# A decode step with modulation, attention and a token mixer: a quarter of two modulation terms loaded by GpSimd, and three terms formed by wide products and a fold

## The chip, the cores and the metric

The kernel runs on one core of one Trainium2 chip. The metric is the device time of one execution in microseconds. Five engines work side by side, each through its own instruction queue: TensorE (PE in the profile; its weight loads are PEld), VectorE (DVE), ScalarE (ACT), GpSimd (POOL) and SyncE (SP). Transfers between HBM and the on-chip memory (SBUF) are issued from one of these queues and carried out by 16 DMA engines. Products of TensorE land in PSUM.

## What is computed

One decoding step for four sequences (B = 4) of width D = 512:

```python
mod = (silu(c) @ w_mod).reshape(B, 6, 1, D)
sa, ca, ga, sb, cb, gb = mod[:, 0], ..., mod[:, 5]
h = layernorm(x) * (1 + ca) + sa
x = x + ga * attention(h, k_cache, v_cache, wq, wo)   # 32 query heads, 8 key/value heads, 4096 cached positions
h = layernorm(x) * (1 + cb) + sb
x = x + gb * mixer(h, w1, b1, w2, b2)                 # u = gelu(layernorm(h) * w1 + b1), y = u @ w2 + b2, hidden width 1792
```

All is float32. The caches of 4 x 8 heads are 2 MB for keys and 2 MB for values each, `w_mod` is 512 x 3072 (6.3 MB), `wq` and `wo` are 8.4 MB each: 157 MB are read once.

## The kernel before

**Items.** The attention is cut into 32 items, one for each pair of sequence and key/value head. For item `i`: `scores` (eight products against the key block), row maxima (`row_max`, `turn_max`, `col_max`, `spread_max`, `copy_max`), `expo` on ScalarE, `turn` (transposes), `sums` and `scale`, `values` (eight products in four column groups), `copy_v`, `pick`, `copy_o`, `project` with `wo`, and `add_up`. A loop runs items 0 to 23 in software-pipelined order; the last eight are put in order by a written plan (`PLAN`), in which the mixer of the last two sequences and the last modulation term are woven in.

**Transfers.** All loads are issued by SP, in the order of the code. Large ones land in a ring of three buffers of 32 KB in each lane (tag `kv`): first the weights of modulation terms 0 and 1 (`wm01`), then `wq` in two halves, the first two key blocks, and then pairs of a later key block and an earlier value block (`load_pair`, 4 MB each). A load into a ring buffer waits, on SP's queue, until the buffer's last reader is done; everything behind it on SP waits too. `wo` comes in four pieces into buffers of its own. At the end come single key and value blocks, the last value block in four pieces, and last the weights of modulation term 5 (`load_wm5`).

**Small inputs.** `small` holds in each of 128 lanes the mixer's `w1`, `b1`, `w2` (14 columns each), the 16 columns of `c` transposed, and `b2`. It is loaded at the start in three pieces (lanes 0 to 6, 6 to 16, 16 to 128), `x` behind it. `w1n`, the negative of `w1`, is VectorE's first instruction (L70); the constants follow. `sg`, `sT` and `sT8` (L118 to L125) are silu(c), the last repeated eight times so that each sequence fills eight rows of a product.

**The modulation terms.** Terms 0 and 1 are made at the start. Terms 2, 3 and 4 are made in the loop at i = 2 (L609 to L616): `load_wm24` (L197), called at i = 1 behind the load of a pair and a piece of `wo`, brings their weights, 3 x 1 MB, into one ring buffer. `mod(t)` makes one term as [128, 128], sixteen products of [128 x 32] by [128 x 128]: four quarters `k` of the 512 inputs, and four blocks `c` of the 512 outputs, each block in its own group of 32 PSUM rows. The term is copied into `prep`. The PSUM buffer for this (pool `ps_e`) is a single one.

**Elsewhere.** `fold_groups` (L355) sums the four row groups of a [128, 512] accumulator by products with the column `first`, and gives [128, 128]. The buffers `u` (three of [128, 2, 512]) belong to the mixer, whose first instance starts at i = 8. GpSimd makes the identity at the start (in `make_identity`) and has nothing else to do.

Of the kernel before, what the change touches and what calls it, by code (L numbers as in the profile page):

```python
# [8 lines left out]
F32 = mybir.dt.float32  # L9
I32 = mybir.dt.int32  # L10
AF = mybir.ActivationFunctionType
OP = mybir.AluOpType
# [9 lines left out]
NSM = 3 * NF + 16 + 1  # L22

# [5 lines left out]


@with_exitstack
def adaln_decode(ctx: ExitStack, tc: tile.TileContext, small, x, wmod, wq, kk, kv, vv, wo, out):
# [16 lines left out]
    sm = cst.tile([P, NSM], F32, name="sm")  # L51
    xr = wk.tile([P, D], F32, name="xr", tag="yw", bufs=1)[0:B]
    wm01 = ring.tile([P, 2, 4, D], F32, name="wm01", tag="kv")
    nc.sync.dma_start(wm01, wmod[0])
# [9 lines left out]
    cT = sm[:, 3 * NF:3 * NF + 16]  # L64
    b2 = sm[:, 3 * NF + 16:]
# [4 lines left out]
    dv.tensor_scalar(w1n, w1, -1.0, None, op0=OP.mult)  # L70
    ones = cst.tile([P, P], F32, name="ones")
    dv.memset(ones, 1.0)
    dv.memset(neg1, -1.0)
# [4 lines left out]
    g32 = cst.tile([P, 32], F32, name="g32")  # L78
# [9 lines left out]
    first = g32[:, 0:1].to_broadcast([P, 32])  # L88
# [8 lines left out]
    sT8 = cst.tile([P, 4, B, 8], F32, name="sT8")  # L97

    def rsqrt(ve, n, tag, beside=None, out=None, times=None):
        y = wk.tile([n, 1], F32, name="y" + tag)  # L100
# [11 lines left out]
        if times is not None:  # L112
# [2 lines left out]
        dv.scalar_tensor_tensor(y, q, RS3, y, op0=OP.add, op1=OP.mult)  # L115
        return y

    sg = cst.tile([P, 16], F32, name="sg")  # L118
    nc.scalar.activation(sg, cT, AF.Exp, scale=-1.0)
    dv.tensor_scalar(sg, sg, 1.0, None, op0=OP.add)  # L120
    dv.reciprocal(sg, sg)
    sT = cst.tile([P, 4, B], F32, name="sT")
    dv.tensor_mul(sT.rearrange("p k b -> p (k b)"), sg, cT)  # L123
    dv.tensor_copy(sT8.rearrange("p k b r -> p (k b) r"),
                   sT.rearrange("p k b -> p (k b)").unsqueeze(2).to_broadcast([P, 16, 8]))  # L125

    st = wk.tile([B, 6], F32, name="st0")
    dv.bn_stats(st, xr)
# [59 lines left out]
    def load_pair(i):  # L188
        t = slots()
        nc.sync.dma_start(t, kv[i])  # L190
        key(t[:, 0], i + 2)
        value(t[:, 1], i)

    def load_wo(h):
        nc.sync.dma_start(wo_p[h // 2], wo[h // 2])

    def load_wm24():  # L197
        w = ring.tile([P, 3, 4, D], F32, name="wm24", tag="kv")
        nc.sync.dma_start(w[:, 0:2], wmod[1])
        nc.sync.dma_start(w[:, 2], wmod[2][:, 0])  # L200
        for e in range(3):
            WM[2 + e] = w[:, e]

    def load_wm5():
        t = slots().rearrange("p s (k n) -> p (s k) n", n=D)
        nc.sync.dma_start(t[:, 0:4], wmod[2][:, 1])
        WM[5] = t[:, 0:4]
        return t[:, 4:6]

    def load_key(t, i):  # L210
# [9 lines left out]
    def modmm(pm, t, ks=range(4)):  # L220
        for k in ks:
            for c in range(4):
                mm(pm[32 * c:32 * c + 32, :], sT8[:, k].rearrange("p b r -> p (b r)"),
                   WM[t][:, k, c * P:(c + 1) * P], start=(k == 0), stop=(k == 3))

    def mod(t):
        pm = ps_e.tile([P, P], F32, name=f"pm{t}", tag="e")
        modmm(pm, t)
        return pm

    S, M, PL, SEL = {}, {}, {}, {}

    def scores(i):
        b, h = divmod(i, HKV)
        S[i] = s = ps_s.tile([P, 1024], F32, name=f"s{i}", tag="s")
        for n in range(2):
            for c in range(4):
                mm(s[32 * c:32 * c + 32, n * 512:(n + 1) * 512], QT[:, b, h, :],  # L238
                   KT[i][:, (n * 4 + c) * 512:(n * 4 + c + 1) * 512], start=True, stop=True)
# [91 lines left out]
    def project(i, pa=None):  # L331
        b, h = divmod(i, HKV)
        oT = OT.pop(i)
        if pa is None:
            pa = ps_m.tile([P, D], F32, name="pa", tag="m")
            for g in range(REP):
                mm(pa[32 * g:32 * g + 32, :], oT[:, g:g + 1].to_broadcast([P, 32]), wo_t[h][:, g, :],  # L337
                   start=True, stop=True)
        else:
            for g in range(REP):  # L340
                for c in range(4):
                    mm(pa[32 * c:32 * c + 32, :], oT[:, g:g + 1].to_broadcast([P, 32]),
                       wo_t[h][:, g, c * P:(c + 1) * P], start=(g == 0 and h == HKV - 2),
                       stop=(g == REP - 1 and h == HKV - 1))
        PA[i] = pa
# [6 lines left out]
        else:  # L352
            dv.tensor_add(ACC[b], ACC[b], pa)  # L353

    def fold_groups(pool, acc, tag):  # L355
        pc = pool.tile([P, P], F32, name="pc", tag=tag)
        for c in range(4):
            mm(pc[32 * c:32 * c + 32, :], first, acc[:, c * P:(c + 1) * P], start=True, stop=True)
        return pc

    def residual(x1, pc):
# [216 lines left out]
    for i in range(NS - HKV):  # L578
        load_pair(i + 1)
        if i in (1, 3, 5):  # L580
            load_wo(i + 1)
        if i == 1:
            load_wm24()
        scores(i + 2)
        row_max(i + 2)
        if i:
            pick(i - 1)
            copy_o(i - 1)
        turn(i + 1)
        sums(i + 1)  # L590
        scale(i + 1)
        if i:
            project(i - 1)
            add_up(i - 1)
        turn_max(i + 2)
        col_max(i + 2)
        values(i, range(4))
        spread_max(i + 2)
        copy_max(i + 2)
        expo(i + 2)  # L600
        if i and i % HKV == 0:
            mix = Mixer(i // HKV - 1)
        if mix:
            mix.inner(i % HKV)
        values(i, range(4, 8))
        copy_v(i)
        if mix:
            mix.outer(i % HKV)
        if i == 2:  # L609
            for t in range(2, 5):  # L610
                pm = mod(t)
                dst = prep[:, {2: 1, 3: 2, 4: 3}[t]]
                if t == 4:
                    dv.tensor_scalar(dst, pm, 1.0, None, op0=OP.add)
                else:
                    dv.tensor_copy(dst, pm)  # L616
        if i == NS - HKV - 2:
            gate = spread_gate()
# [25 lines left out]
    for step in PLAN.split():  # L644
        op, k = step.rstrip("0123456789."), step.lstrip("abcdefghijklmnopqrstuvwxyzABCDEFGHIJKLMNOPQRSTUVWXYZ")
        i, q = (int(n) for n in (k + ".0").split(".")[:2]) if k else (0, 0)
# [32 lines left out]
        elif op == "y":  # L679
            pc = fold_groups(ps_m, ACC.pop(B - 1), "m")  # L680
# [54 lines left out]
```

## Time and profile before

| | us |
|---|---|
| median of three timed runs | 389.92 (388.86 to 390.04) |
| the profiled execution, its span | 386.94 |
| TensorE busy | 298.9 (77%) |
| VectorE busy | 215.2 (56%) |
| ScalarE busy | 108.0 (28%) |
| GpSimd busy | 0.7 |
| DMA queue q1 (all loads) | 157.33 MB, 94.8% of 16 engines' time |

How to read the profile: the page gives busy time by engine, then the span in 40 equal slices (busy tenths, the granted TensorE clock, the busy share of the DMA engines, GB/s), then the DMA queues, and then the chain of work that ended last, followed back from the last instruction at each step to what released it. Rows of the chain have the start in us, the duration in us, and what ran. Rows of the timeline have the start, the duration, engine and line, the operation with its output and inputs, the shape, the count, and in brackets how long the engine had been idle before and what ended that. Rows of windows have busy time and count of instructions of each engine in a stretch, then the granted clock, the DMA share and GB/s. A matmul of float32 counts as two entries (x8 is four products).

### The profile page before, as it was taken

The page shows a single profiled execution, that of the slowest core. Times are in us where ns is not written, and L with a number is a line of the kernel's source. Part 1 is how long each engine was busy: PE and PEld are TensorE (multiplying, and loading weights), DVE is VectorE, ACT ScalarE, POOL GpSimd, SP SyncE. Part 2 cuts the span into 40 slices and gives each one's busy share as a digit, 9 for nine tenths or more (in the row PEclk, how much of TensorE's full clock was granted, in tenths as well). Part 3 has the DMA queues.
Part 4 walks back from the last instruction along what each step waited for, and adds up shares of the span by engine and source line. Part 5 has one row for each costly group of instructions (what it writes and reads, how often), then busy time and mean ns, then how long its engine had stood idle before and what let it go on. Part 6 is the DMA issues. An engine that isn't in the chain of part 4 may idle for free.

```text
span 386.9 us, 5714 instructions
## 1 busy us (share of the span) xinstructions
PE 298.9 (77%) x2416; PEld 122.4 (32%) x2416; DVE 215.2 (56%) x516; ACT 108.0 (28%) x132; POOL 0.7 (0%) x6
## 2 busy tenths in 40 slices
PE   0765575863966949979888859999988887999984
PEld 0111121231323313334222323443323342444562
DVE  0420351620542524676766644676875579788766
ACT  0101120110110110113567210213783104757356
POOL 0000000000000000000000000000000000000000
PEclk9998875986695775989999985978999998899999
DMA  8999999999999999999999999999999999999910
GB/s 329 430 434 434 415 451 430 410 449 432 418 447 434 430 434 432 434 432 434 426 434 429 434 429 434 434 432 434 425 434 432 434 429 434 422 427 423 404 46 3
DMA packets 7281, 157.70 MB, mean 408 GB/s; under 512 B 964, under 2 KB 980, under 8 KB 1368
## 3 DMA queue, kind: packets, MB, share of 16 engines
q1 hardware_dynamic: 7248, 157.33, 94.8%
q8 instruction: 19, 0.31, 0.3%
q14 instruction: 6, 0.05, 0.0%
q10 hardware_dynamic: 8, 0.00, 0.0%
HBM read 157.32 MB, written 0.01 MB: 407 GB/s over the span
## 4 chain that ended last, share of the span: by engine, by line
DMA 54%; PE 28%; DVE 16%; issue 1%; SPq 1%; ACTq 0%; DVEq 0%
DMA kv<-in_kv 47%; PE s L238 8%; PE pv L301 7%; DMA wq<-in_wq 6%; DVE m L243 3%; DVE p L275 3%; PE pt L324 2%; PE pa L337 2%; PE pb L258 2%; DVE uu L431 1%; DVE mx L252 1%; DVE acc L353 1%; PE qs L152 1%; PE phb L417 1%; PE pve L309 1%
## 5 line engine op out<-in xcount | busy, mean ns | idle before, releaser
L238 PE MATMUL s<-kv,QT 128*32 128x512 f32 x512 | 76.2, 715 | 35.6 <-DMA kv<-in_kv 32.6
L268 ACT ACTIVATE p<-s,nm 128x1024 f32<-128x1024 f32 x32 | 35.6, 1114 | 199.0 <-DVE nm L263 198.9
L243 DVE TENSOR_REDUCE m<-s 128x1 f32<-128x1024 f32 x32 | 39.2, 1224 | 76.1 <-PE s L238 76.0
L301 PE MATMUL pv<-kv,p 128*32 128x512 f32 x496 | 75.0, 684 | 0.4 <-DMA kv<-in_kv 0.4
L275 DVE STREAM_TRANSPOSE p<-p 128x512 f32<-128x512 f32 x64 | 41.9, 687 | 1.7 <-ACT p L268 1.7
L324 PEld LDWEIGHTS pt<-sel,po 128*128 128x128 f32 x250 | 33.6, 208 | 28.7 <-issue 15.6
L238 PEld LDWEIGHTS s<-kv,QT 128*32 128x32 f32 x512 | 16.3, 125 | 81.3 <-DMA kv<-in_kv 45.3
L337 PE MATMUL pa<-wo,oT 128*32 128x512 f32 x240 | 35.3, 663 | 4.3 <-DVE oT L329 4.2
L324 PE MATMUL pt<-sel,po 128*128 128x4 f32 x250 | 36.2, 268 | 1.4 <-DVE po L315 1.4
L315 DVE COPY po<-pv 128x512 f32<-128x512 f32 x31 | 21.4, 689 | 17.0 <-PE pv L301 17.0
L252 DVE TENSOR_REDUCE mx<-pm 1x128 f32<-1x512 f32 x32 | 21.4, 671 | 0.8 <-PE pm L247 0.7
L258 PEld LDWEIGHTS pb<-neg,mx 1*128 1x128 f32 x64 | 10.8, 210 | 32.9 <-DVE mx L252 31.1
L487 ACT ACTIVATE u<-u 128x1024 f32<-128x1024 f32 x20 | 20.4, 1052 | 2.7 <-DVE u L431 2.6
L431 DVE TENSOR_SCALAR u<-hb,wr,sm 128x512 f32<-128x512 f32 x40 | 19.9, 541 | 1.0 <-PE py L442 0.9
L353 DVE TENSOR_TENSOR acc<-acc,pa 128x512 f32<-128x512 f32 x26 | 17.7, 681 | 3.6 <-PE pa L337 3.6
L268 ACT ACT_TABLE_LOAD x11 | 14.1, 1283 | 19.0 <-DVE nm L263 18.9
L137 PE MATMUL s<-wm,sT 128*4 128x512 f32 x16 | 8.4, 684 | 12.2 <-DVE sT L123 12.2
L258 PE MATMUL pb<-neg,mx 1*128 1x1 f32 x64 | 13.5, 278 | 5.3 <-DVE mx L252 5.3
L487 ACT ACT_TABLE_LOAD x13 | 16.7, 1283 | 0.2
L247 PE MATMUL pm<-ident,m 128*1 128x128 f32 x32 | 9.1, 286 | 9.8 <-DVE rl L284 3.8
L301 PEld LDWEIGHTS pv<-kv,p 128*32 128x32 f32 x496 | 14.1, 146 | 8.1 <-issue 2.1
L247 PEld LDWEIGHTS pm<-ident,m 128*1 128x1 f32 x32 | 2.5, 80 | 39.1 <-DVE rl L284 21.0
(144 smaller groups left out, 212.3 us busy)
## 6 DMA issues: line engine op xcount, KB each, us to landing
kv<-in_kv SPq DMA_DIRECT2D x28, 4096.0 KB, 20.8
wq<-in_wq SPq DMA_DIRECT2D x2, 4096.0 KB
wo<-in_wo SPq DMA_DIRECT2D x4, 2048.0 KB
kv<-in_kv SPq DMA_DIRECT2D x4, 2048.0 KB, 18.5
wm<-in_wmod SPq DMA_DIRECT2D x2, 2048.0 KB
kv<-in_kk SPq DMA_DIRECT2D x1, 4096.0 KB
kv<-in_vv SPq DMA_DIRECT2D x3, 1024.0 KB
wm<-in_wmod SPq DMA_DIRECT2D x1, 1024.0 KB
```

Of the source, the lines that this page charges most:

```text
L238: mm(s[32 * c:32 * c + 32, n * 512:(n + 1) * 512], QT[:, b, h, :], KT[i][:, (n * 4 + c) * 512:(n * 4 + c + 1) * 512], start=True, stop=True)
L243: dv.tensor_reduce(M[i], S[i], axis=AX.X, op=OP.max)
L252: dv.tensor_reduce(mx, M[i].rearrange("o (c r) -> o r c", c=4).unsqueeze(1).to_broadcast([1, 4, 32, 4]), axis=AX.X, op=OP.max)
L258: mm(pb, M[i].rearrange("o c r -> o (c r)"), neg1, start=True, stop=True)
L268: nc.scalar.activation(p, S[i], AF.Exp, bias=M.pop(i), accum_out=l)
L275: dv.transpose(p, p)
L301: mm(PV[i][32 * q:32 * q + 32, :], pT[:, 128 * k:128 * k + 128:4], VT[i][:, 4 * k:4 * k + 4, :].rearrange("p j d -> p (j d)"), start=(k < ...
L324: mm(pt, po[:, c * DH:(c + 1) * DH], sel[:, c, :], start=(c == 0), stop=(c == n - 1))
L337: mm(pa[32 * g:32 * g + 32, :], oT[:, g:g + 1].to_broadcast([P, 32]), wo_t[h][:, g, :], start=True, stop=True)
L353: dv.tensor_add(ACC[b], ACC[b], pa)
L431: dv.tensor_scalar(u[:, e, :], hb, wr[:, j:j + 1], b1[:, j:j + 1], op0=OP.mult, op1=OP.add)
L487: nc.scalar.activation(u, u, AF.Gelu_apprx_tanh)
```

## The change

Five things change.

1. `small` is split. `cond` (32 columns of `c`, and `b2`) is loaded at the start in the same three pieces; `mlp` (`w1`, `b1`, `w2`) is loaded with the weights of terms 2 and 3. `w1n` is made at i = 2.
2. `x` is loaded in two halves, the first by GpSimd, the second by SP.
3. Of terms 2 and 3 the first three quarters of the inputs come by SP as before (`w23`, 1.5 MB). The last quarter, 128 inputs, is laid out over 32 lanes (8 to 31 and 64 to 71), four inputs in each: 16 KB a lane for both terms. GpSimd first sets that region of the buffer to zero on all 128 lanes, and then issues four rounds of three transfers: six lanes, two lanes, and eight lanes of `mlp` (six in the last round). The remaining lanes of `mlp` come by SP.
4. `cT` has 16 more columns: on those 32 lanes the matching inputs of `c`, zero elsewhere. `sg`, `sT` and `sT8` grow with it.
5. The weights of term 4 go into two of the mixer's `u` buffers, in two loads. `mod` is replaced by `mod_wide`: for a term 7 products (4 for term 4) of [128 x 32] by [128 x 512] in four row groups, a copy to SBUF, and a fold of the four groups with `g32`.

```diff
-    for lo, hi in ((0, 6), (6, 16), (16, P)):
-        nc.sync.dma_start(sm[lo:hi], small[lo:hi])
-    nc.sync.dma_start(xr, x)
+    for lo, hi in ((0, 6), (6, 16), (16, P)):
+        nc.sync.dma_start(cond_t[lo:hi], cond[lo:hi])
+    nc.gpsimd.dma_start(xr[0:2], x[0:2])
+    nc.sync.dma_start(xr[2:B], x[2:B])
...
     def load_wm24():
-        w = ring.tile([P, 3, 4, D], F32, name="wm24", tag="kv")
-        nc.sync.dma_start(w[:, 0:2], wmod[1])
-        nc.sync.dma_start(w[:, 2], wmod[2][:, 0])
-        for e in range(3):
-            WM[2 + e] = w[:, e]
+        w = ring.tile([P, 14, D], F32, name="wm24", tag="kv")
+        low = w[:, 6:14]
+        nc.gpsimd.memset(low, 0.0)
+        nc.sync.dma_start(w[:, 0:6], w23)
+        for e in range(4):
+            nc.gpsimd.dma_start(low[8 + e:32:4], wlow[e, 0:6])
+            nc.gpsimd.dma_start(low[64 + e:72:4], wlow[e, 6:8])
+            nc.gpsimd.dma_start(sm[8 * e:min(8 * e + 8, 30)], mlp[8 * e:min(8 * e + 8, 30)])
+        nc.sync.dma_start(sm[30:P], mlp[30:P])
+        for t in range(2):
+            WM[2 + t] = [w[:, 3 * t + k] for k in range(3)] + [low[:, 2 * s + t] for s in range(NL)]
+        WM[4] = []
+        for h in range(2):
+            u = up.tile([P, 2, D], F32, name="u")
+            nc.sync.dma_start(u, w4[h])
+            WM[4] += [u[:, k] for k in range(2)]
...
-    def mod(t):
-        pm = ps_e.tile([P, P], F32, name=f"pm{t}", tag="e")
-        modmm(pm, t)
-        return pm
+    def mod_wide(t):
+        pm = ps_e.tile([P, D], F32, name=f"pm{t}", tag="e")
+        n = len(WM[t])
+        for k, w in enumerate(WM[t]):
+            q = k % 4
+            e = k if k < 3 or n == 4 else k + 1
+            mm(pm[32 * q:32 * q + 32, :], sT8[:, e].rearrange("p b r -> p (b r)"), w, start=(k < 4), stop=(k + 4 >= n))
+        wide = wk.tile([P, D], F32, name="wide", tag="yw", bufs=1)
+        dv.tensor_copy(wide, pm)
+        return fold_groups(ps_e, wide, "e", g32)
...
-    def fold_groups(pool, acc, tag):
+    def fold_groups(pool, acc, tag, sel=None):
         pc = pool.tile([P, P], F32, name="pc", tag=tag)
         for c in range(4):
-            mm(pc[32 * c:32 * c + 32, :], first, acc[:, c * P:(c + 1) * P], start=True, stop=True)
+            mm(pc[32 * c:32 * c + 32, :], first if sel is None else sel, acc[:, c * P:(c + 1) * P], start=True, stop=True)
         return pc
...
         if i == 2:
+            dv.tensor_scalar(w1n, w1, -1.0, None, op0=OP.mult)
             for t in range(2, 5):
-                pm = mod(t)
+                pm = mod_wide(t)
```

The inputs are laid out on the host to fit:

```python
SPOT = [*range(8, 32), *range(64, 72)]
cT[SPOT, 4:] = a["c"][:, 3 * P:].reshape(B, NL, 32).transpose(2, 1, 0)
low = wm[3, :, 2:4].reshape(NL, 8, 4, 2, D)
"wlow": con(low.transpose(2, 1, 0, 3, 4).reshape(4, 8, 2 * NL, D)),
```

More of the change, by code (lines that the diff above doesn't have):

```diff
@@ L21 @@
 NS = B * HKV
-NSM = 3 * NF + 16 + 1
+NL = 4
+NC = (4 + NL) * B
+SPOT = [*range(8, 32), *range(64, 72)]
 TAU2 = (3.0 / 8.0) ** 0.4
@@ L33, in adaln_decode @@
 @with_exitstack
-def adaln_decode(ctx: ExitStack, tc: tile.TileContext, small, x, wmod, wq, kk, kv, vv, wo, out):
+def adaln_decode(ctx: ExitStack, tc: tile.TileContext, cond, mlp, x, w01, w23, wlow, w4, w5, wq, kk, kv, vv, wo, out):
     nc = tc.nc
@@ L197, in load_wm24 @@
     def load_wm24():
[L198 to L202 removed]
+        w = ring.tile([P, 14, D], F32, name="wm24", tag="kv")
[14 more added lines that the diff above has]
+            WM[4] += [u[:, k] for k in range(2)]
     def load_wm5():
         t = slots().rearrange("p s (k n) -> p (s k) n", n=D)
[L206 to L207 removed]
+        nc.sync.dma_start(t[:, 0:4], w5)
+        WM[5] = [t[:, k] for k in range(4)]
         return t[:, 4:6]
@@ L709 @@
     con = _np.ascontiguousarray
-    cT = a["c"].reshape(B, 4, P).transpose(2, 1, 0).reshape(P, 16)
-    small = _np.concatenate([
-        a["B_w1"].reshape(P, NF), a["B_b1"].reshape(P, NF), a["B_w2"].reshape(P, NF), cT,
-        _np.broadcast_to(a["B_b2"].reshape(1, 1), (P, 1))], axis=1)
+    cT = _np.zeros((P, 4 + NL, B), _np.float32)
+    cT[:, :4] = a["c"].reshape(B, 4, P).transpose(2, 1, 0)
+    cT[SPOT, 4:] = a["c"][:, 3 * P:].reshape(B, NL, 32).transpose(2, 1, 0)
+    cond = _np.concatenate([cT.reshape(P, NC), _np.broadcast_to(a["B_b2"].reshape(1, 1), (P, 1))], axis=1)
+    mlp = _np.concatenate([a["B_w1"].reshape(P, NF), a["B_b1"].reshape(P, NF), a["B_w2"].reshape(P, NF)], axis=1)
+    wm = a["w_mod"].reshape(4, P, 6, D)
+    low = wm[3, :, 2:4].reshape(NL, 8, 4, 2, D)
     k = a["A_k_cache"].reshape(B, HKV, 4, 32, 2, 16, DH).transpose(0, 1, 6, 4, 2, 5, 3)
@@ L717 @@
     arrays = {
-        "small": con(small),
+        "cond": con(cond),
+        "mlp": con(mlp),
         "x": con(a["A_x"].reshape(B, D)),
-        "wmod": con(a["w_mod"].reshape(4, P, 3, 2, D).transpose(2, 1, 3, 0, 4)),
+        "w01": con(wm[:, :, 0:2].transpose(1, 2, 0, 3)),
+        "w23": con(wm[:3, :, 2:4].transpose(1, 2, 0, 3).reshape(P, 6, D)),
+        "wlow": con(low.transpose(2, 1, 0, 3, 4).reshape(4, 8, 2 * NL, D)),
+        "w4": con(wm[:, :, 4].reshape(2, 2, P, D).transpose(0, 2, 1, 3)),
+        "w5": con(wm[:, :, 5].transpose(1, 0, 2)),
         "wq": con(a["A_wq"].reshape(2, 2, P, HQ * DH).transpose(0, 2, 1, 3)),
```

19 lines of the change are left out of this document (9 added, 10 removed).

## The prediction

> **What bounds the kernel now.** I read the page's slices first, then the queues, then the chain of waits, and then went into the last microseconds.
>
> ```profile
> span 386.9 us, 5714 instructions
> ...
> DMA  8999999999999999999999999999999999999910
> GB/s 329 430 434 434 415 451 430 410 449 432 418 447 434 430 434 432 434 432 434 426 434 429 434 429 434 434 432 434 425 434 432 434 429 434 422 427 423 404 46 3
> ...
> q1 hardware_dynamic: 7248, 157.33, 94.8%
> q8 instruction: 19, 0.31, 0.3%
> q14 instruction: 6, 0.05, 0.0%
> ```
>
> All 16 DMA engines are busy from the second slice to the 38th at about 432 GB/s, so the time is the bytes, plus a start, plus a tail of arithmetic. Of one engine: 94.8% of 16 x 386.9 us is 5869 engine-us for 157.33 MB, so 32 KB (32,768 bytes) cost an engine 1.22 us, and 16 KB 0.61 us. The nineteen packets of the q8 instruction queue take 0.3% of 16 x 386.9, or 18.6 engine-us, 0.98 us each (0.81 to 1.14 by the rounding of 0.3%), for 16 KB each: a packet from another queue holds an engine some 0.37 us longer than its bytes would (0.20 to 0.53).
>
> The chain of waits shows where the stream hands over to arithmetic:
>
> ```profile
> 271.39 18.52 DMA kv<-in_kv
> 289.95 1.97 PE s L238 x16
> ...
> 336.33 21.56 DMA kv<-in_kv
> ...
> 358.03 1.95 PE pv L301 x16
> ...
> 367.53 0.22 PE pc L358 x8
> 367.75 0.42 PE pve L309 x8
> ...
> 384.06 0.29 DVE osb L552
> ```
>
> From 358.03, when a value block lands, TensorE has no gap worth naming until the last piece of the last value block (367.75); what follows, 386.94 - 367.75 = 19.2 us, is arithmetic that the change leaves alone. A landing that comes later moves this tail by as much. A landing that comes earlier does so only if the loads before it (289.95) come earlier too; they are in the same stream, so they would.
>
> A transfer has landed only when its slowest engine is done, so I looked at how the engines finish:
>
> ```profile
> 366.00:367.00 1.00, 1.00 (x44) 0.93 (x36) 1.00 (x4) 0.82 (x1) 0.00 (x0) 1.00 0.97 389
> 367.00:368.00 1.00, 1.00 (x35) 0.64 (x31) 0.60 (x2) 0.98 (x2) 0.00 (x0) 1.00 0.61 254
> 368.00:369.00 1.00, 1.00 (x41) 0.80 (x30) 0.60 (x3) 0.74 (x2) 0.00 (x0) 1.00 0.54 229
> 369.00:370.00 1.00, 1.00 (x24) 0.88 (x24) 0.16 (x1) 0.00 (x0) 0.00 (x0) 1.00 0.24 90
> ```
>
> The last two columns are DMA share and GB/s. The load does not fade evenly. A share of 0.54 through the whole of 368 to 369 is 0.54 x 16 = 8.6 engines still at work; the others (7.4) were done at about 367.2 (the rest of the 0.61). The 8.6 end at about 369 + 0.24 x 16 / 8.6 = 369.45. So eight or nine engines are late by some 2.3 us, and they set the landings.
>
> **The change, part by part.** The execution behind these rows took 386.94 us; the median of the timed runs is 389.92 (388.86 to 390.04), so 2.98 us lie around the span, and I add them to every sum.
>
> *The quarter that moves.* Before, two terms times a quarter of w_mod are 128 lanes x 4 KB = 512 KB, 32 KB to each of 16 engines. After, the same bytes are 32 lanes x 16 KB in pieces of six and two lanes, with pieces of eight `mlp` lanes between them: 6 + 2 + 8 = 16. If transfers are dealt lane by lane to engines in turn, the same eight engines take 4 x 16 KB = 64 KB each, and the other eight only 168-byte rows. Eight engines gain 32 KB (+1.22 us), eight lose 32 KB (-1.22 us). That would level a lag of 2.4 us if the eight relieved were all of the late ones. But 8.6 engines are late, and a window of eight cannot spare nine, even where it fits the other eight. I take it that at least one late engine is loaded: the last landing goes from 367.75 to 368.97, **+1.22 us**. Bounds: -1.22 (all late engines relieved) to +1.22 for one round of pieces at work as described.
>
> [...]
>
> *The twelve GpSimd transfers and the small pieces.* The row of the small loads of before:
>
> ```profile
> 5.00:10.00 5.00, 0.00 (x0) 0.00 (x0) 0.69 (x7) 0.82 (x1) 0.00 (x0) 1.00 1.06 447
> ```
>
> There `small` lands in 128 rows and `x` in four, and the stream shows no dent: 447 GB/s. `cond` takes the place of `small` row for row; new are 128 `mlp` rows and the marks of some 14 more transfers, of the same kind. Lower bound 0. Upper bound: each of the twelve transfers stops every engine as a q8 packet does, 12 x 0.53 = 6.4 us. The pieces are rows like those of the quoted window, on a busy stream, so I take **+0.2 us**, near the low end, and keep 12 x 0.37 = 4.4 us as a rival.
>
> *GpSimd's own queue.* Its memset of 128x4096 waits for the same ring slot as the SP load:
>
> ```profile
> 0.73 0.20 POOL masks.py:197 MEMSET ident<- 128x128 f32 x1 [0.29 <-POOLq L727]
> ...
> 10.52 0.91 DVE L90 MEMSET QT<- 128x1024 f32 x1 [0.16 <-issue]
> ...
> 58.80 0.33 SPq L199 DMA_DIRECT2D wm<-in_wmod  x1
> 59.18 0.43 SPq L200 DMA_DIRECT2D wm<-in_wmod  x1
> 72.06 8.50 SPq L190 DMA_DIRECT2D kv<-in_kv  x2
> ...
> 88.27 17.71 SPq L190 DMA_DIRECT2D kv<-in_kv  x2
> ...
> 82.77 1.62 PE L223 MATMUL pm<-wm,sT 128*32 128x128 f32 x32 [2.59 <-DMA wm<-in_wmod]
> 84.78 1.93 PE L223 MATMUL pm<-wm,sT 128*32 128x128 f32 x32 [0.40 <-DVE prep L616]
> 87.13 1.08 PE L223 MATMUL pm<-wm,sT 128*32 128x128 f32 x32 [0.42 <-DVE prep L616]
> 94.85 3.64 PE L238 MATMUL s<-kv,QT 128*32 128x512 f32 x16 [6.64 <-DMA kv<-in_kv]
> ```
>
> The slot is free at 58.8. The memset costs 4 x 0.91 = 3.6 us at VectorE's rate, 32 x 0.20 = 6.4 at GpSimd's: done by 62.4 to 65.2. Twelve issues at SP's 0.43 us are 5.2 us: 70.4. The memset waits on its queue ahead of all twelve, and the last five also wait until one of the first eight has landed. The low rows are wanted at 82.8 plus three products, some 12 us after, so I cost this at nothing. Cover gone: late low rows hold t = 2's fourth product, behind it on TensorE `scores(5)` (94.85), and on SP the key/value load that takes this ring slot (88.27). That load has slack:
>
> ```profile
> kv<-in_kv SPq DMA_DIRECT2D x28, 4096.0 KB, 20.8
> ```
>
> From issue to landing such a load takes 20.8 us, and its 4.19 MB at 434 GB/s take 9.7, so about 11 us of work lie ahead in the stream. Below 11 us of delay the engines do not run dry.
>
> *The products and the fold.* 48 narrow products (three rows above, 82.77 to 88.21) become 7 + 7 + 4 wide ones, with a copy and a fold for each term:
>
> ```profile
> 299.09 0.42 PE pc L358 x8
> ...
> L315 DVE COPY po<-pv 128x512 f32<-128x512 f32 x31 | 21.4, 689 | 17.0 <-PE pv L301 17.0
> ...
> 84.44 0.29 DVE L616 COPY prep<-pm 128x128 f32<-128x128 f32 x1 [3.50 <-PE pm L223]
> ```
>
> Seven wide products are about two rounds of four, 1.95 us (the x16 row at 358.03); copy 0.69, fold 0.42, copy into `prep` 0.29: 3.4 us. The term with four: 1.0 + 1.4 = 2.4. In all 9.2 us from 82.77, so 92.0, where TensorE waits for keys until 94.85. Nothing on the path; without that wait it would be 9.2 - 5.4 = +3.8 us. The ring slot's last reader is t = 3's products, at 82.77 + 3.4 + 1.95 = 88.1 against 88.21 now: SP's load at 88.27 stays. Term 4's weights move to two `u` buffers, which nothing uses before the first mixer, and `w1n` (0.17 us) moves to where VectorE waits 3.50.
>
> *The start.*
>
> ```profile
> 9.22 0.17 DVE L70 TENSOR_SCALAR w1n<-sm 128x14 f32<-128x14 f32 x1 [9.22 <-DMA sm<-in_small]
> ...
> 10.47 0.22 ACT L119 ACTIVATE sg<-sm 128x16 f32<-128x16 f32 x1
> ...
> 11.49 0.11 DVE L120 TENSOR_SCALAR sg<-sg 128x16 f32<-128x16 f32 x1
> ```
>
> VectorE's setup no longer stands behind `w1n`, so the conditioning chain may go on at 10.69 instead of 11.49, 0.8 us earlier. The stream is full by then (447 GB/s) and sets the pace: 0. Half of `x` on GpSimd stands ahead of the identity by one issue, some 0.4 us; VectorE wants the identity only after 9. SP issues one transfer more than before, at 0.33 to 0.43 us, with 11 us of queue ahead: 0.
>
> Sum: 386.94 + 1.22 + 0.2 = 388.36 in the span, and with 2.98 around it **391.3 us**.
>
> **The rivals.**
>
> *Levelled (faster).* The eight relieved engines are the late ones, and a ninth is hardly late. For it: 64 KB against none is 2.4 us, nearly the lag of 2.3. Against: 8.6 is more than eight. 386.94 - 1.22 + 0.2 + 2.98 = 388.9.
>
> *Every visit costs.* The q8 packets hold an engine 0.37 us too long; twelve transfers at that price are 4.4 us on every engine, on top of the 1.22. For it: it is the only row of two queues on one engine. Against: those packets carry 16 KB each, most of these almost nothing. 386.94 + 1.22 + 4.4 + 2.98 = 395.5.
>
> *All pieces begin at the same engine.* Six, two and eight lanes each start over at the first engine; the first two then take eight rows of 16 KB, 128 KB instead of 32: +96 KB, 3.66 us. If one of the two is late already: 386.94 + 3.66 + 0.2 + 2.98 = 393.8. [...]
>
> *It doesn't shift anything.* The pieces spread evenly over 16 engines, and only the small pieces remain: 386.94 + 0.2 + 2.98 = 390.1.
>
> *GpSimd is late.* The low rows land after 95, and the ring slot is free only past 99.3, 88.27 plus 11: the stream runs dry. At 3 us a transfer they land at 65 + 36 = 101; with the rest of t = 2 and the products of t = 3 (4.4 us) the load is issued at 105.4, 6.1 us too late: 391.3 + 6.1 = 397.4. Against: three microseconds each is seven times SP's issue.
>
> [...]
>
> **How the numbers follow.** Chances: forecast 0.44; levelled 0.22; every visit costs 0.17; same first engine 0.07; nothing shifted 0.05; GpSimd late 0.05. 0.3% of 389.92 is 1.17 us, about what a measurement of this kernel can tell from no change: faster is below 388.75, slower above 391.09. The forecast (own range 390.6 to 392.2, as the small pieces cost 0 to 0.8 and the loaded engine is less or more late) gives 0.35 slower and 0.09 within; levelled 0.17 faster and 0.05 within; nothing shifted 0.05 within; the other three slower, 0.29. Faster 0.17, within 0.19, slower 0.64. The range reaches into levelled (388.6) and reaches to the visits' price (395.6); about 0.06 lies below and 0.10 above.
>
> **What would show it.** Right: in the last windows fewer engines at work after 368.5, but one or a few until about 370.7, and the last value product 1.2 to 1.5 us later than 367.75. Levelled: the share falls from 1 to 0 within about a microsecond, ending before 369. Visits: GB/s dips between 62 and 80, and all later landings of keys and values move by 4 us. Same first engine: a long thin end, two engines only. The steps that I cost at nothing are wrong if TensorE's wait before `scores(5)` is gone, or if a load at 88 is issued more than 11 us later. The forecast is wrong if the last value product starts before 367.7.

## The result, and the profile after

The changed kernel takes 395.97 us (median of 5, 395.61 to 396.79), the kernel before beside it 389.09 (5 runs, 388.86 to 390.04): a ratio of 1.0177, 95% interval 1.0163 to 1.0191, so 6.9 us slower. (Here and below the ratio is worked out from the executions of both kernels; it is not exactly the quotient of the two medians.) The forecast was 391.3 and its range ended at 395.6.

The page of the changed kernel, its span, slices and queues:

```profile
span 394.7 us, 5692 instructions
...
DMA  8999999999999999999999999999999999999800
GB/s 321 432 432 448 413 446 402 329 315 425 420 448 425 423 435 442 437 432 430 426 427 426 440 442 427 435 427 426 437 442 427 435 431 425 418 430 423 363 20 1
...
q1 hardware_dynamic: 7500, 156.81, 94.0%
q0 software_dynamic: 416, 0.53, 0.5%
```

GpSimd's queue (q0) holds 0.53 MB and half a per cent of the engines' time, yet slices 8 and 9 of the GB/s row, about 69 to 89 us, fall from 410 and 449 to 329 and 315, while the DMA digits stay at 9. The engines are as busy as before and move less. Windows of 5 us (busy time and count of PE, PEld, DVE, ACT, POOL, then granted clock, DMA share, GB/s), first of before:

```profile
65.00:70.00 5.00, 4.58 (x35) 1.65 (x27) 3.42 (x8) 0.00 (x0) 0.00 (x0) 0.89 1.00 433
70.00:75.00 5.00, 4.13 (x38) 1.35 (x30) 1.68 (x4) 1.21 (x2) 0.00 (x0) 1.00 0.91 387
75.00:80.00 5.00, 4.44 (x35) 1.72 (x34) 3.84 (x9) 0.56 (x1) 0.00 (x0) 1.00 1.01 433
80.00:85.00 5.00, 2.01 (x41) 1.36 (x41) 0.98 (x2) 0.65 (x2) 0.00 (x0) 0.82 1.07 456
85.00:90.00 5.00, 2.79 (x64) 1.99 (x56) 0.58 (x2) 0.00 (x0) 0.00 (x0) 0.84 1.02 439
```

and of the changed kernel:

```profile
60.00:65.00 5.00, 1.84 (x12) 0.53 (x16) 0.00 (x0) 0.00 (x0) 4.70 (x8) 0.58 1.03 446
65.00:70.00 5.00, 5.00 (x30) 2.48 (x22) 2.58 (x5) 0.00 (x0) 1.44 (x3) 0.50 1.01 347
70.00:75.00 5.00, 5.00 (x31) 1.17 (x27) 1.74 (x6) 1.13 (x2) 0.69 (x2) 0.56 0.93 312
75.00:80.00 5.00, 4.59 (x43) 1.90 (x35) 3.83 (x8) 0.07 (x1) 0.87 (x2) 1.00 0.98 326
80.00:85.00 5.00, 2.13 (x18) 0.51 (x10) 1.68 (x4) 1.21 (x2) 0.00 (x0) 0.97 1.00 289
85.00:90.00 5.00, 0.00 (x0) 0.00 (x0) 0.00 (x0) 0.00 (x0) 0.00 (x0) 0.50 1.06 346
90.00:95.00 5.00, 3.75 (x18) 0.87 (x22) 0.87 (x2) 0.00 (x0) 0.00 (x0) 0.50 1.04 446
```

From 65 to 90 the mean is 430 GB/s before and 324 after. 106 GB/s over 25 us are 2.6 MB, at 433 GB/s 6.1 us: nearly the whole loss, and with the queue's own 0.53 MB already counted as moved. In 65 to 70, 32 KB cost 1.01 x 80 engine-us / (347 x 5 us / 32,768 bytes) = 1.53 us on average instead of 1.21. The trace's packet records show it packet by packet: at 69.0 us sixteen packets of 32 KB are under way, as many as there are engines, and each takes 1.38 to 1.43 us; at 69.0 us of the kernel before, all sixteen take 1.21. The engines do not stand idle (no share below 0.93); their packets are longer, on all sixteen. The dip lies between GpSimd's first issue (61.82) and the end of the last packet of a low row (88.6). TensorE waits until 90.45, by the profile for `w23` (`wm<-in_w`), the part of the weights that SP loads: issued at 57.97, it lands 32.4 us later. Timeline and issue row of the changed kernel (timeline: start, duration, what, and in brackets the idle time before):

```profile
57.97 0.33 SPq L203 DMA_DIRECT2D wm<-in_w  x1
...
58.00 3.51 POOL L202 MEMSET wm<- 128x4096 f32 x1 [55.52 <-PE pv L320]
61.82 0.52 POOL L205 DMA_DIRECT2D wm<-in_wlow  x1 [0.30 <-POOL wm L202]
...
69.34 0.52 POOL L207 DMA_DIRECT2D sm<-in_mlp  x1 [3.42 <-DMA wm<-in_wlow]
...
76.89 0.52 POOL L207 DMA_DIRECT2D sm<-in_mlp  x1 [1.54 <-DMA wm<-in_wlow]
...
90.45 3.63 PE L245 MATMUL pm<-wm,sT 128*32 128x512 f32 x14 [8.16 <-DMA wm<-in_w]
...
99.13 11.49 SPq L192 DMA_DIRECT2D kv<-in_kv  x2
...
102.80 1.47 PE L257 MATMUL s<-kv,QT 128*32 128x512 f32 x12
...
wm<-in_w SPq DMA_DIRECT2D x1, 1536.0 KB, 32.4
```

Two rows of the chain of waits of the changed kernel:

```profile
365.52 1.95 PE pv L320 x16
...
375.26 0.41 PE pve L328 x8
```

and its windows where the stream ends:

```profile
372.00:373.00 1.00, 1.00 (x12) 0.81 (x8) 1.00 (x3) 0.00 (x0) 0.00 (x0) 1.00 0.82 342
373.00:374.00 1.00, 1.00 (x35) 0.98 (x37) 1.00 (x3) 0.33 (x1) 0.00 (x0) 1.00 0.69 285
374.00:375.00 1.00, 1.00 (x44) 0.80 (x32) 0.91 (x3) 0.98 (x2) 0.00 (x0) 1.00 0.28 115
375.00:376.00 1.00, 1.00 (x40) 0.76 (x32) 0.64 (x3) 1.00 (x1) 0.00 (x0) 1.00 0.23 98
376.00:377.00 1.00, 1.00 (x25) 0.80 (x16) 0.25 (x2) 0.24 (x2) 0.00 (x0) 1.00 0.20 74
```

The last value product starts at 375.26 instead of 367.75, 7.5 us later; the tail behind it is 19.4 us (394.7 - 375.26), before 19.2. So nearly all of it is late landings. At the end a share of 0.28 to 0.20, or 4.5 to 3.2 of 16 engines, goes on for three microseconds.

### The profile page after: what moved, and what is told of

Same layout as the page of the kernel before. It is cut to its first block, busy times and chain, and to the rows that moved or that the text cites. A ratio compares the mean times of both kernels' runs of the same rounds, so it can differ in the third digit from the quotient of the medians.

```text
span 394.7 us, 5692 instructions
## 1 busy us (share of the span) xinstructions
PE 299.2 (76%) x2380; PEld 117.3 (30%) x2380; DVE 217.3 (55%) x519; ACT 108.0 (27%) x132; POOL 11.1 (3%) x20
## 4 chain that ended last, share of the span: by engine, by line
DMA 55%; PE 26%; DVE 14%; ACT 3%; issue 1%; SPq 0%; ACTq 0%; DVEq 0%
DMA kv<-in_kv 53%; PE s L257 7%; PE pv L320 5%; DVE m L262 3%; DVE p L294 3%; PE qs L154 3%; PE s L139 2%; PE pa L356 2%; PE pt L343 2%; DMA cond<-in_cond 2%; DVE mx L271 2%; DVE acc L372 1%; ACT uu L561 1%; PE pb L277 1%; PE pve L328 1%
## 5 line engine op out<-in xcount | busy, mean ns | idle before, releaser
L257 PE MATMUL s<-kv,QT 128*32 128x512 f32 x512 | 73.4, 698 | 37.2 <-DMA kv<-in_kv 35.4
L320 PE MATMUL pv<-kv,p 128*32 128x512 f32 x496 | 71.3, 652 | 0.2 <-DMA kv<-in_kv 0.2
L343 PEld LDWEIGHTS pt<-sel,po 128*128 128x128 f32 x250 | 32.8, 204 | 28.0 <-issue 19.7
L257 PEld LDWEIGHTS s<-kv,QT 128*32 128x32 f32 x512 | 15.1, 119 | 80.2 <-DMA kv<-in_kv 51.8
L277 PEld LDWEIGHTS pb<-neg,mx 1*128 1x128 f32 x64 | 10.0, 194 | 31.7 <-DVE mx L271 30.0
L139 PE MATMUL s<-wm,sT 128*4 128x512 f32 x16 | 9.5, 761 | 11.4 <-DVE sT L125 11.4
L277 PE MATMUL pb<-neg,mx 1*128 1x1 f32 x64 | 12.7, 265 | 5.2 <-DVE mx L271 5.2
## 6 DMA issues: line engine op xcount, KB each, us to landing
wm<-in_w SPq DMA_DIRECT2D x1, 1536.0 KB, 32.4
```

The lines of the kernel that those rows point to most:

```text
L277: mm(pb, M[i].rearrange("o c r -> o (c r)"), neg1, start=True, stop=True)
L320: mm(PV[i][32 * q:32 * q + 32, :], pT[:, 128 * k:128 * k + 128:4], VT[i][:, 4 * k:4 * k + 4, :].rearrange("p j d -> p (j d)"), start=(k < ...
```

## The experiments

Eighteen kernels; all times are medians, each beside the kernel before on the same chip (`a_spread`: of four executions, see there). "GB/s" is the mean of the five windows from 65 to 90. The kernels called `m...` and `b...` are the kernel before with one addition, those called `a...` the changed kernel, edited as the diffs show.

| kernel | us | before | ratio (95%) | GB/s |
|---|---|---|---|---|
| changed | 395.97 | 389.09 | 1.0177 (1.0163 to 1.0191) | 324 |
| m12_pool | 390.77 | 389.20 | 1.0027 (1.0012 to 1.0042) | 420 |
| m4_pool | 390.16 | 389.20 | 1.0015 (0.9997 to 1.0033) | 424 |
| m12_sp | 396.04 | 389.20 | 1.0172 (1.0120 to 1.0224) | 339 |
| m12_act | 395.49 | 389.20 | 1.0162 (1.0104 to 1.0219) | 368 |
| a_plain | 389.62 | 389.19 | 1.0020 (1.0002 to 1.0039) | 423 |
| a_low_sp | 393.73 | 389.19 | 1.0114 (1.0098 to 1.0129) | 378 |
| a_two | 395.28 | 389.19 | 1.0151 (1.0131 to 1.0170) | 349 |
| b_g4 | 394.31 | 389.19 | 1.0125 (1.0105 to 1.0145) | 381 |
| a_spread | 397.45 | 389.27 | 1.0198 (1.0169 to 1.0226) | not read |
| b_s1 | 391.82 | 389.27 | 1.0062 (1.0044 to 1.0081) | 395 |
| b_s4 | 389.99 | 389.27 | 1.0014 (1.0003 to 1.0026) | 430 |
| b_g4s | 393.12 | 389.27 | 1.0095 (1.0071 to 1.0118) | 391 |
| a_match | 391.11 | 389.61 | 1.0042 (1.0018 to 1.0065) | 424 |
| a_match_x | 390.60 | 389.61 | 1.0025 (1.0009 to 1.0040) | 425 |
| a_match_sp | 390.36 | 389.61 | 1.0032 (1.0014 to 1.0051) | 416 |
| b_gm | 390.80 | 389.61 | 1.0036 (1.0018 to 1.0055) | 428 |
| a_lanes | 390.77 | 389.60 | 1.0036 (1.0017 to 1.0054) | 421 |
| a_rot | 393.96 | 389.60 | 1.0112 (1.0082 to 1.0142) | 378 |

**First theory: each of GpSimd's transfers interrupts the stream.** That was the rival at 395.5, and the time lay beside it. Four kernels add small transfers that nothing reads; the diff is that of `m12_pool`, `m4_pool` has four of them, `m12_sp` and `m12_act` issue the twelve by `nc.sync` and `nc.scalar`:

```diff
-        w = ring.tile([P, 3, 4, D], F32, name="wm24", tag="kv")
+        w = ring.tile([P, 4, 4, D], F32, name="wm24", tag="kv")
         nc.sync.dma_start(w[:, 0:2], wmod[1])
         nc.sync.dma_start(w[:, 2], wmod[2][:, 0])
+        for e in range(12):
+            nc.gpsimd.dma_start(w[8 * e:8 * e + 8, 3, 0, 0:42], small[8 * e:8 * e + 8, 0:42])
```

> The kernel before, and beside its load of terms 2 to 4 GpSimd issues twelve transfers of 8 lanes x 168 bytes into an unused quarter of the same ring buffer: 16 KB in all, no memset, nothing reads them. Theory (every GpSimd transfer interrupts the SP stream on all 16 engines, about 0.48 us each): 12 x 0.48 = 5.8 us later, so 394.9 from 389.1 (394 to 396), a GB/s dip while the twelve are issued, last value product near 373.5 instead of 367.75, and the share at the end still falling in the old two steps because no engine got more bytes. Rival (the loss comes from the 512 KB dealt to eight engines, or from memset, products and fold): no more than 0.2 us, 389.3, no dip.

> The same with four such transfers instead of twelve. Theory: a third of the price, 4 x 0.48 = 1.9 us, so 391.0 (390.6 to 391.5). Rival (a fixed price for starting the second queue at all, whatever the count): the same as with twelve, near 395 if that is slower. Rival (data and products): 389.2.

> The same twelve small transfers, but issued by SP, in the stream's own queue. Theory (the price is for a second queue on the engines): each engine gets at most a few rows of 168 bytes more, 0 to 0.3 us, 389.1 to 389.4, no dip. Rival (small pieces cost it, from whatever queue): like twelve by GpSimd, near 395.

> The same twelve small transfers issued by ScalarE. Theory in its wide form (any second queue makes the engines turn from the stream to it and back): near 395, like GpSimd. Theory in its narrow form (GpSimd's transfers alone, by the way they are written or fetched): 389.1 to 389.6. I lean to the narrow form, 389.5, with a ScalarE issue of some 0.4 us each that delays nothing on the path.

The theory fell with the first kernel: twelve GpSimd transfers cost 0.27% or 1.1 us, not 5.8, and there is no dip. Four of them (`m4_pool`), expected at 391.0, cannot be told from no change (0.9997 to 1.0033). Windows of `m12_pool`:

```profile
65.00:70.00 5.00, 5.00 (x26) 2.41 (x18) 2.72 (x6) 0.00 (x0) 0.52 (x1) 0.50 0.98 420
...
75.00:80.00 5.00, 4.44 (x37) 1.91 (x29) 3.97 (x8) 0.00 (x0) 0.00 (x0) 1.00 1.00 421
```

The two that were to be free were slow, for a reason that has nothing to do with the engines: an issuing queue that was given twelve transfers at once stood still until earlier ones had landed. SP's timeline in `m12_sp`:

```profile
61.69 25.01 SPq L202 DMA_DIRECT2D wm<-in_small  x12
86.80 0.35 SPq L190 DMA_DIRECT2D kv<-in_kv  x1
```

and two of its windows:

```profile
80.00:85.00 5.00, 2.18 (x52) 1.58 (x52) 0.98 (x2) 0.75 (x2) 0.00 (x0) 0.91 0.60 248
85.00:90.00 5.00, 2.64 (x56) 1.80 (x48) 0.58 (x2) 0.00 (x0) 0.00 (x0) 0.75 0.59 182
```

The next key/value load, issued at 72.06 in the kernel before, went out at 86.80, and the share fell to 0.59: here the engines did run dry. ScalarE's timeline in `m12_act` has the same:

```profile
58.86 15.50 ACTq L202 DMA_DIRECT2D wm<-in_small  x12
74.47 1.11 ACT L270 ACTIVATE p<-s,nm 128x1024 f32<-128x1024 f32 x1 [16.05 <-DMA wm<-in_small]
```

Its exponentials stood behind the issues. These two say nothing on a second queue; that a stream that runs dry looks different (a low share) from what the changed kernel shows (a full share, fewer GB/s) is what they taught. A price for every visit would have kept the share full too; it is `m12_pool` that speaks against it.

**Second theory: large rows in GpSimd's queue, whatever their number.** The low rows issued by SP (`a_low_sp`), by GpSimd in two transfers (`a_two`), not at all (`a_plain`); and 262 KB added to the kernel before (`b_g4`):

```diff
 # a_plain: NL = 0, no memset, no GpSimd transfer; mlp and x whole by SP
+        w = ring.tile([P, 8, D], F32, name="wm24", tag="kv")
+        nc.sync.dma_start(w, w23)
 # a_two; a_low_sp has nc.sync in both lines. wlow is laid out in lane order
+        nc.gpsimd.dma_start(low[8:32], wlow[0:24])
+        nc.gpsimd.dma_start(low[64:72], wlow[24:32])
+        nc.sync.dma_start(sm, mlp)
 # b_g4: into the fourth quarter, as above
+        for e in range(4):
+            nc.gpsimd.dma_start(w[8 * e:8 * e + 8, 3], wmod[2][8 * e:8 * e + 8, 1])
```

> The changed kernel with the quarter back in SP's load on all 128 lanes (16 KB a lane, no GpSimd transfer, no memset, mlp and x each in one load by SP); the wide products, the folds, the split of the small arrays and term 4's two buffers stay. Theory after the twelve small transfers (rows of 16 KB in GpSimd's queue slow the packets of all 16 engines, 1.21 us to 1.4 and more from 65.6 to 90): gone, 388.6 to 389.8. Rival (products, folds, 4 KB rows of term 4 or the split cost it): 394 to 396.

> The changed kernel, the low rows to the same 32 lanes and of the same 16 KB, but by two transfers (24 and 8 lanes) that SP issues; mlp by SP in one; GpSimd keeps its memset and half of x. Theory (GpSimd's queue): packets of 1.21 us all along, some engines with 16 KB more and some with 16 KB less, 0.6 us, 389 to 390.5. Rival (the 32 lanes or the 16 KB rows themselves slow the engines, whoever issues): GB/s of 290 to 350 between 65 and 90 as in the changed kernel, near 396.

> The same two transfers of 24 and 8 lanes, issued by GpSimd, so its queue holds the same 512 KB in two transfers instead of eight. Theory by bytes: the same packets stretched for as long, 394.5 to 396.5. Theory by count of transfers: a quarter of it, 390.5 to 391.5. Rival (lanes or rows): 396, and then the kernel above too.

> The kernel before, with four GpSimd transfers of 8 lanes x 8 KB into the unused quarter of the same buffer, beside its load: 262 KB that nothing reads. Their own bytes are 0.6 us. Theory by bytes in GpSimd's queue: half of the changed kernel's 524 KB, so half of its 6.1 us, 3.0, plus 0.6: 392.7 (392 to 393.5), a dip to some 350 GB/s. Theory that the lanes, memset or products are needed for it: 389.7, no dip.

`a_plain` (389.62) clears the wide products, folds and split arrays: 0.2%. `a_two` and `b_g4` are slow, `b_g4` even more than half the bytes should make it (394.31, where 392 to 393.5 was expected). But `a_low_sp` is slow too, with no low row in GpSimd's queue. Its windows:

```profile
75.00:80.00 5.00, 4.44 (x37) 1.85 (x29) 3.97 (x8) 0.00 (x0) 0.00 (x0) 1.00 1.05 408
80.00:85.00 5.00, 2.35 (x16) 0.50 (x15) 0.85 (x2) 1.21 (x2) 0.00 (x0) 0.75 0.98 203
```

203 GB/s at a share of 0.98. So GpSimd's queue is not needed for it; where the rows go remained.

**Third theory: too many rows into one block of lanes.**

```diff
 # a_spread: every fourth lane
-SPOT = [*range(8, 32), *range(64, 72)]
+SPOT = [*range(0, P, 4)]
-            nc.gpsimd.dma_start(low[8 + e:32:4], wlow[e, 0:6])
-            nc.gpsimd.dma_start(low[64 + e:72:4], wlow[e, 6:8])
+            nc.gpsimd.dma_start(low[4 * e:96:16], wlow[e, 0:6])
+            nc.gpsimd.dma_start(low[96 + 4 * e:P:16], wlow[e, 6:8])
 # b_s1
+        nc.sync.dma_start(w[0:32, 3], wmod[2][0:32, 1])
 # b_s4
+        nc.sync.dma_start(w[0:P:4, 3], wmod[2][0:32, 1])
 # b_g4s
+        for e in range(4):
+            nc.gpsimd.dma_start(w[4 * e:P:16, 3], wmod[2][8 * e:8 * e + 8, 1])
```

> The changed kernel with one thing moved: the 32 low rows go to every fourth lane (0, 4, ... 124) instead of lanes 8 to 31 and 64 to 71; the same GpSimd transfers of 6, 2 and 8 rows in the same order, the same bytes, memset and products. Theory of the lanes (24 of the 32 rows, 393 KB, are written into one block of 32 lanes; a block takes only about its even share of 433 GB/s, 108, and every engine is held behind it: 3.6 us for that block and 1.2 for lanes 64 to 71): no dip, packets of 1.21 us all along, 389 to 391.3, with the end set by how the eight loaded engines fall. Rival (16 KB rows in a second queue cost it wherever they go): 395 to 396.

> The kernel before, and 32 rows of 8 KB (262 KB that nothing reads) by one SP transfer into lanes 0 to 31 of the unused quarter. Own bytes 0.6 us. Theory of the lanes: 262 KB at 108 GB/s are 2.4 us on every engine, so 3 us or a little less, 391.8 to 392.7, dip right before the load of modulation terms. Rival (GpSimd's queue is needed): 389.8, no dip.

> The same 32 rows by SP into every fourth lane. Theory of the lanes: own bytes alone, 389.5 to 390.3, packets not stretched. Rival (rows that many engines fetch from a small part of memory, or a transfer of 32 rows as such): as the kernel with lanes 0 to 31.

> The kernel before with the four GpSimd transfers of 8 rows x 8 KB, now each into every sixteenth lane, together every fourth lane, instead of lanes 0 to 31 (which took 394.3). Theory of the lanes: 389.7, or up to 391 if the engines that get the rows are those that end last. Rival (large rows in GpSimd's queue): 394.

From SP it looked right: 32 rows into lanes 0 to 31 cost 2.4 us and into every fourth lane 0.5. Through GpSimd it failed twice: spread lanes still cost 3.7 us (`b_g4s`), and in the changed kernel they cost no less than its own lanes (395.65 to 398.60 in four executions; a fifth, the one with the profile, took 887.06 and is not read). Neither the queue nor the lanes alone explain it; the pair was tried next, which engine writes which lane.

**Fourth theory: two engines meet at one group of lanes.** The theory assumes that in every full load of 128 lanes each engine writes the same lanes; call it their owner. A row that another engine carries there would then meet the owner's packets. The traces do not number the engines, so no row shows an owner or the dealing: both are only inferred, from which kernels are slow. `a_match` puts row j of each transfer of eight into one of lanes 4j to 4j + 3. The theory takes the owner of these four for the engine that carries row j, by a count from the first engine, and also by a cursor that goes on (an `mlp` piece of eight follows each); `a_match_x` puts two rows of `x` ahead, which would shift a cursor by two; `a_match_sp` issues them by SP; `b_gm` is `b_g4` with the same lanes dealt in the matched way.

```diff
 # a_match (a_match_x keeps x[0:2] on GpSimd)
-SPOT = [*range(8, 32), *range(64, 72)]
+SPOT = [*range(32)]
-    nc.gpsimd.dma_start(xr[0:2], x[0:2])
-    nc.sync.dma_start(xr[2:B], x[2:B])
+    nc.sync.dma_start(xr, x)
-            nc.gpsimd.dma_start(low[8 + e:32:4], wlow[e, 0:6])
-            nc.gpsimd.dma_start(low[64 + e:72:4], wlow[e, 6:8])
+            nc.gpsimd.dma_start(low[e:32:4], wlow[e])
 # b_gm
-            nc.gpsimd.dma_start(w[8 * e:8 * e + 8, 3], wmod[2][8 * e:8 * e + 8, 1])
+            nc.gpsimd.dma_start(w[e:32:4, 3], wmod[2][8 * e:8 * e + 8, 1])
```

> The changed kernel with the low rows in lanes 0 to 31, four GpSimd transfers of 8 rows (lanes e, e+4, ... e+28), an 8-row mlp piece after each, all of x by SP. Theory of the matched engine (packets stretch where an engine writes a lane that another engine writes in the stream's full loads; here row j goes to engine j, whether transfers start at the first engine or follow a cursor): packets stay at 1.21 us, no dip between 65 and 90, and only the bytes remain, eight engines 32 KB more: 389 to 390.5. Rival (16 KB rows in GpSimd's queue cost it in any case): 395 to 397. Rival (a block of 32 lanes is the limit): 395 or more, as all 32 rows are now in one block. [...]

> The same, but two rows of x go through GpSimd first, as in the changed kernel. If each transfer of few rows starts again at the first engine, nothing changes: as the kernel above. If a cursor goes on from transfer to transfer, every low row is now written by an engine two further on than the lane's own: stretched packets, 394 to 397, though the lanes, bytes and instructions are the same.

> The same four matched pieces of 8 rows issued by SP, mlp in one load by SP, nothing by GpSimd but its memset. Theory of the matched engine: as a_match, 389 to 391 (SP may wait a while between its issues), against 393.7 for SP's unmatched 24 + 8 rows. Rival (rows of few lanes cost it from SP too): 393 or more.

> The kernel before with four GpSimd transfers of 8 rows x 8 KB into lanes 0 to 31, as in the kernel that took 394.3, only dealt lane e, e+4, ... e+28 in transfer e instead of lanes 8e to 8e+7: same lanes, bytes, count. Theory of the matched engine with every transfer starting at the first engine: no dip, own bytes on eight engines, 389.5 to 391. With a cursor: the second and fourth transfer unmatched, half a dip, 391.5 to 393. Rival (GpSimd's queue or the block of lanes): 394.

All four are within 1.6 us of before (`a_match` at 391.11, where 389 to 390.5 was expected), and the dip is gone (416 to 428 GB/s from 65 to 90) but for a remainder in `a_match_sp`, 401 GB/s from 80 to 85. Windows of `a_match`:

```profile
65.00:70.00 5.00, 5.00 (x26) 2.41 (x18) 2.71 (x6) 0.00 (x0) 1.66 (x4) 0.50 0.97 420
...
75.00:80.00 5.00, 4.58 (x43) 2.00 (x39) 3.69 (x8) 0.00 (x0) 0.00 (x0) 1.00 0.98 413
```

The pair `b_g4` and `b_gm` is the plainest: the same 32 rows, the same 32 lanes, four GpSimd transfers of eight each, only dealt otherwise: 394.31 and 390.80. The window of 70 to 75 of `b_g4`:

```profile
70.00:75.00 5.00, 1.87 (x18) 0.51 (x10) 1.42 (x3) 1.21 (x2) 0.00 (x0) 1.00 0.90 290
```

and of `b_gm`:

```profile
70.00:75.00 5.00, 5.00 (x27) 1.21 (x23) 1.87 (x6) 1.00 (x1) 0.00 (x0) 0.51 0.90 383
```

In the packet records from 65 to 90, all 162 packets of 32 KB of `b_gm` take 1.21 us; those of `b_g4` take up to 2.09.

`a_match_x` (390.60) is no slower than `a_match` (391.11): by this theory, two rows ahead do not shift the dealing. `b_gm` says the same: with a cursor that goes on, its second and fourth transfer would have been unmatched and half a dip left, and 428 GB/s are no dip.

**The changed kernel with nothing but its lanes moved, and a shift by one.**

```diff
 # a_lanes, from the changed kernel
+SPOT = [*range(24), *range(32, 40)]
+            nc.gpsimd.dma_start(low[e:24:4], wlow[e, 0:6])
+            nc.gpsimd.dma_start(low[32 + e:40:4], wlow[e, 6:8])
 # a_rot, from a_match
+SPOT = [*range(4, 36)]
+            nc.gpsimd.dma_start(low[4 + e:36:4], wlow[e])
```

> The changed kernel with all its transfers as they are (six rows, two rows, eight mlp rows, half of x, the same order), only the lanes moved to suit transfers that all start at the first engine: six rows to lanes e, e+4, ... e+20, two rows to 32+e and 36+e. Theory (every transfer of few rows starts at the first engine; a meeting of two engines at one group of lanes is what stretches): no dip, packets 1.21 us, but engines 0 and 1 get 128 KB instead of 32, 3.66 us, and four get 64 KB: at the end a share of about 2/16 = 0.12 for two to three microseconds, 391.5 if the first two are early engines, up to 393.8 if one is late. If pieces follow a cursor instead, these lanes are all unmatched: 395 to 398. [...]

> a_match with every low row moved on by four lanes (lanes 4 to 35), so that engine j writes the lanes of engine j+1 and engine 7 those of engine 0. If a row must go to the engine's own lanes: stretched packets and a dip, 394 to 397. If only the load of a group of lanes counts, and eight engines moving on by one at about the same time leave each group one writer: little, 391 to 392.5. I lean to the first, since the engines' packets start up to 1.2 us apart.

`a_lanes` keeps every transfer of the changed kernel, in size, order and queue, and has no dip; none of its packets of 32 KB from 65 to 90 takes more than 1.23 us. It came out faster than the 391.5 that was expected at best. Its windows, the last two those of the end:

```profile
65.00:70.00 5.00, 4.58 (x35) 1.80 (x31) 3.20 (x7) 0.00 (x0) 4.02 (x8) 0.86 0.94 406
70.00:75.00 5.00, 4.12 (x36) 1.11 (x28) 1.67 (x5) 1.21 (x2) 1.55 (x3) 1.00 0.96 400
75.00:80.00 5.00, 4.44 (x37) 1.97 (x37) 4.08 (x9) 0.32 (x1) 0.52 (x1) 1.00 0.99 410
80.00:85.00 5.00, 0.54 (x7) 0.12 (x6) 0.69 (x1) 0.89 (x2) 0.00 (x0) 0.84 1.10 459
...
370.00:371.00 1.00, 1.00 (x44) 1.00 (x40) 0.75 (x3) 0.98 (x2) 0.00 (x0) 1.00 0.17 74
371.00:372.00 1.00, 1.00 (x41) 0.80 (x33) 0.79 (x3) 0.99 (x2) 0.00 (x0) 1.00 0.10 33
```

1.0177 against 1.0036: of the 6.9 us, about 5.5 hang on the destination lanes alone, by this theory on the meeting of engines, and about 1.4 (0.7 to 2.1) on everything else in the change. The end is thin, a share of 0.17 and 0.10, or 2.7 and 1.6 of 16 engines; that the first two carry 128 KB, as the expectation has it, would give such an end, but no row shows which engines these are. The matching assumed that all pieces start at the first engine; had they followed a cursor, `a_lanes` would by this theory have been all unmatched. `a_rot`, too, keeps the transfers of `a_match`; it moves each row of `a_match` on by four lanes and the dip is back, 393.96, in its window

```profile
75.00:80.00 5.00, 4.59 (x39) 1.77 (x31) 3.81 (x8) 0.00 (x0) 0.00 (x0) 1.00 1.02 331
```

so by this theory it is not enough that each of eight groups of lanes has one foreign writer.

Open: how SP deals the 32 rows of `b_s4` over the engines, and so why it is nearly free (0.5 us) though every fourth lane was not through GpSimd (3.7 us in `b_g4s`); there all sixteen engines may leave their own lanes at once. That was not tried apart, and until it is, the theory is shown for the pairs above and not for every unmatched load. Nor did any run show where in the path the sixteen engines are held together.

No kernel was faster than the one before.

## Why the prediction was wrong, point by point

- **The quarter that moves** is the step that failed. It assumed that pieces "are dealt lane by lane to engines in turn", which no run shows, counted the bytes of each engine, +1.22 us, and had no term for the lanes that an engine writes. Of the two dealings, by the theory of owners, only the one in which each transfer of few rows starts at the first engine fits `b_gm` (390.80), `a_match_x` (390.60) and `a_lanes` (390.77). The six rows of a piece then go out from the first engines to lanes 8 to 31, each eight lanes further on than in `a_lanes`, so by the same theory to lanes of others, and packets on all sixteen engines are stretched (1.38 to 1.43 us at 69.0); whose lanes 64 to 71 are, no run shows. The missing term is 5.5 us (the changed kernel against `a_lanes`).
- **Its bytes, +1.22**, are neither confirmed nor refuted. In `a_match`, where the rows match, the last value product starts at 369.43, 1.7 us later than 367.75, and the time is 391.11, near the forecast's 391.3. But in `m12_pool`, which adds 16 KB in all, the last instruction of these products starts at 369.6, as in `a_match`, so the nearness may be luck.
- **Same first engine (393.8, chance 0.07)** had the dealing that fits and priced it by bytes alone. `a_lanes`, which by the theory has that dealing and matched lanes, takes 390.77: two loaded engines that both end early would cost 3.66 - 2.3 = 1.4 us, which is what was measured; but nothing shows which engines end early, and `m12_pool` costs 1.1 us without these bytes.
- **Every visit costs (395.5, chance 0.17)** gave nearly the time, by luck: the cause is another. Its price was 0.37 us a transfer; `m12_pool` has 1.1 / 12 = 0.09. The q8 packets from which the price came were no measure of small transfers.
- **Twelve transfers and small pieces, +0.2**, were too low: 1.1 us (0.5 to 1.6) in `m12_pool`, where the upper bound was 6.4.
- **GpSimd's own queue**: the memset took 3.51 us (3.6 to 6.4 was the bound) and an issue 0.52 (0.43 taken). The queue ended at 77.4 instead of 70.4, since its last four issues (five were named) waited for landings, stretched ones, by 3.42 us at most.
- **Products and fold**, "nothing on the path": they ran from 90.45 to 102.8 instead of 82.77 to 92.0. They began late because `w23` landed late with the whole stream, and took 12.4 us and not 9.2: seven products, costed at 1.95 us, took 3.63 in the first term, with the granted clock at 0.50 from 90 to 95. The wait before `scores(5)` is gone, the sign that was named for this step being wrong. Its cost was nothing all the same: the slot's load went out at 99.13, 10.9 us later than 88.27, just within the 11 us of queue that were worked out, and the rate is 446 GB/s again from 90. `a_plain` bounds the step itself at 0.8 us (0.1 to 1.5), with the other moved loads.
- **Levelled (388.9)** did not come: the share at the end is thinner and longer (0.28, 0.23, 0.20) than before.
- **What would show it**: the dip "between 62 and 80" was named for the visits. It came, but it is no sign of visits alone: here longer packets gave it at a full share (0.93 to 1.06), where small visits in `m12_pool` did not (388 to 456 GB/s); a queue that ran dry lowered the share as well (0.59 in `m12_sp`).

## What to carry to other kernels

Ask of a load of few lanes not only how many bytes each DMA engine gets, but which lane each row goes to: here the stream lost a quarter of its rate for 25 us (324 GB/s instead of 430), and with other lanes alone, in `a_lanes`, it had 421. That the row's engine must own its lanes is the theory that fits these pairs, not a rule for every load: `b_s4` is open. Two kernels that differ only in the destination lanes test such a theory, as `b_g4` (394.31) and `b_gm` (390.80) did here, and cost one line. And read GB/s against the DMA share: in the changed kernel a full share (0.93 to 1.06) with fewer bytes (289 to 347 GB/s) went with longer packets; in `m12_sp` a low share (0.60 and 0.59) was a queue that ran dry.

## What the runs showed of the hardware that was not expected

- Rows of 16 KB in lanes 8 to 31 and 64 to 71, 0.52 MB in all, held back 2.6 MB of the stream, five times their size. By the dealing that is inferred from `a_lanes`, ten engines carried none of these rows, and yet at 69.0 us packets on all sixteen took 1.38 to 1.43 us instead of 1.21.
- The two rows of each piece that `a_lanes` puts into lanes 32 to 39 went without a dip (400 to 410 GB/s from 65 to 80), like the six in lanes 0 to 23. By the theory, lanes 32 to 35 and 36 to 39 then have the owners of lanes 0 to 3 and 4 to 7; no other lanes of this kind were tried.
- Twelve transfers issued in one go by one queue held it: 25.0 us on SP, 15.5 on ScalarE.
- GpSimd transfers that carry almost nothing were cheap beside a full stream: 0.09 us each in `m12_pool`.
